# Factor transfers on GpSimd's queue, and finished rows gathered by six transfers a chunk

## The chip, the cores and the metric

The kernel runs on one core of a Trainium2 chip. The metric is the device time of one execution in microseconds (us), as the median of several executions. The engines named are PE (TensorE), DVE (VectorE), ACT (ScalarE), POOL (GpSimd) and SP (SyncE, which here only issues transfers). An engine works through its own instructions in order and waits on semaphores that others raise.

## The reference

A dynamic convolution over seven rows with softmaxed weights is followed by a squared-ReLU feed-forward layer:

```python
w = exp(weight_gen - max(weight_gen, -1)); w = w / (sum(w, -1) + 1e-9)   # (8, 4096, 8 heads, 7 taps)
out = einsum('bshk,bskhg->bshg', w, x_unf)      # x_unf: each row of x with the 6 rows before it
h = out.reshape(32768, 192) @ w_in              # w_in 192 x 2048
r = maximum(h, 0)
return (r * r) @ w_out                          # w_out 2048 x 192
```

All inputs and the output are float32.

## The kernel before

The 32768 rows are laid out as 128 partitions of 256 rows. A chunk is four rows of every partition, 512 tokens; there are 64 chunks, and two chunks share one load of x (a group of eight rows plus six rows of halo, lines 156 and 157). The feed-forward products are made from high and low parts in reduced precision, so that each chunk has many passes on PE.

A chunk is worked on in eight steps j = 0 to 7. In each, PE makes two blocks of `ph` (`mm1`, line 523), ACT applies ReLU and square and rounds to the high part `gh` (lines 540, 547, 551), DVE makes the low part `gl` (line 560), and PE adds the second product into four accumulators `acc` (lines 604, 608, 614). The second product lags two steps behind, so that a chunk's accumulators are finished in step 1 of the next chunk. There ACT and DVE take them over in two pairs (lines 649 and 651); PE cannot begin the next chunk's sums before DVE's second addition on line 651 has released the second pair. I call the end of that second addition **the handover**; from one to the next is a **stretch**, which is a chunk's worth of work. A stretch that begins in an even chunk is called even.

Chunks 6 to 62 are the scaled ones (`is_scaled`): their weights are multiplied by powers of two taken from the size of x, and their results are scaled back at the end. What happens around one handover, in the order in which the engines have it:

- The convolution for the chunk after the current one runs on DVE (products on line 387, sums on line 400). Its last step, `turn`, transposes 32x32 blocks (line 488) just after the handover. SP writes the result to a scratch in DRAM (`xd`, four transfers, line 494), waits for it, and reads it back transposed (`xT`, two transfers, line 499). ACT rounds xT to `xh` (line 428) and DVE makes `xl` (line 431), from step 5 on; these feed the next chunk's `mm1`.
- The finished chunk's sums X are transposed by DVE in two parts (lines 661 and 664; before the second part SP moves 64 partitions, line 653, and DVE adds them, line 663). SP then gathers them into rows, `o_sb`: 4 column blocks times 4 quarters for part 0 and 2 times 4 for part 1, so 24 transfers (line 671). They are issued after xT's two.
- One chunk later `close_scaled` multiplies `o_sb` by the closing factor `x_out` twice (line 680) and stores it with four transfers (`put_out` with reads 3, line 98).
- In every even chunk, in step 2, `factor` makes that closing factor for a group: DVE makes a column of 128 numbers (line 282), SP writes it to DRAM (`fd`, line 284) and reads it back in the order of the partitions that `o_sb` has (`x_out`, four transfers, line 288). The first of the four waits for `fd` to have landed. `factor` stands ahead of `turn` in the recorded order, and SP has the transfers in that order.

The order of all engines is recorded by hand (`at`, `spread`, `plan_conv`, and the loop over chunks and steps); nothing reorders it. The last chunk (63) is computed in another way, and the gather of part 1 of chunk 62 is on GpSimd's queue.

Of the kernel before, what the change touches and what calls it, by code (L numbers as in the profile page):

```python
# [30 lines left out]
def kernel(  # L31
# [9 lines left out]
    nc = tc.nc  # L41
# [4 lines left out]
    P = 128  # L46
    Q = 32
    HALO = K - 1
    R = B * S // P
    PPB = S // R  # L50
    TC = 4
# [4 lines left out]
    D1 = 64  # L56
# [32 lines left out]
    def put_out(c, t0, t1, o_sb, reads):  # L89
        rows = slice(rows_of(c) + t0, rows_of(c) + t1)  # L90
        if reads == 0:
            nc.sync.dma_start(out=out.rearrange("(p r) d -> p r d", r=R)[:, rows, :], in_=o_sb[:, t0:t1])
            return
        if reads == 3:
            v = out.rearrange("(q j r) d -> j q r d", q=P // Q, r=R)
            n = Q // (P // Q)
            for k in range(P // Q):
                nc.sync.dma_start(out=v[k * n:(k + 1) * n, :, rows, :], in_=o_sb[k * Q:(k + 1) * Q, t0:t1])
            return
        v = out.rearrange("(q a b r) d -> q b a r d", q=P // Q, a=2 ** reads, r=R)  # L100
        for q in range(P // Q):
            nc.sync.dma_start(out=v[q, :, :, rows, :], in_=o_sb[q * Q:(q + 1) * Q, t0:t1])
# [7 lines left out]
    def is_scaled(c):  # L110
        return FIRST <= c < NCH - 1
# [21 lines left out]
    def rows_of(c):  # L133
        return (c + CPG if c < CPG else c - CPG if c < 2 * CPG else c) * TC
# [144 lines left out]
    def factor(gi):  # L279
        f = att.tile([P, 1], F32, name="x_fac", bufs=2)  # L280
        x_out[gi] = fo = att.tile([P, 1], F32, name="x_out", bufs=3)
        nc.vector.tensor_tensor(out=f, in0=x_pow[gi], in1=v_unroot, op=ALU.mult)
        fd = dram.tile([P, 1], F32, name="fd")
        nc.sync.dma_start(out=fd, in_=f)
        v = fd.rearrange("(q j) e -> j q e", q=P // Q)
        n = Q // (P // Q)
        for k in range(P // Q):
            nc.sync.dma_start(out=fo[k * Q:(k + 1) * Q], in_=v[k * n:(k + 1) * n])

    def peak_w(k):  # L290
        nc.vector.tensor_reduce(
            out=peaks[:, k:k + 1], in_=W[:, 0, 2 * k:2 * k + 2, :].rearrange("p j w -> p (j w)").bitcast(F32),
            axis=AX.X, op=ALU.max, apply_absolute_value=True,
        )
# [7 lines left out]
    def spread_peaks():  # L302
        dm = dram.tile([P, 2], F32, name="dm")
        pk = coef[:, 4:6]
        nc.vector.tensor_reduce(out=pk, in_=peaks.rearrange("p (w k) -> p w k", w=2), axis=AX.X, op=ALU.max)
        nc.sync.dma_start(out=dm, in_=pk)
        nc.sync.dma_start(out=tops, in_=dm.rearrange("p w -> (p w)").rearrange("(o n) -> o n", o=1).broadcast_to([P, 2 * P]))

    def coefficients():
        ts = nc.vector.tensor_scalar  # L310
        top = coef[:, 4:6]
        nc.vector.tensor_reduce(out=top, in_=tops.rearrange("p (q w) -> p w q", w=2), axis=AX.X, op=ALU.max)
        nc.vector.tensor_scalar_max(top, top, W_MIN)
# [15 lines left out]
    def conv_steps(c, on_pe, moving=False):  # L329
# [15 lines left out]
        def denominators(s):  # L345
            if is_scaled(c):
                nc.vector.tensor_scalar(out=s, in0=s, scalar1=1e-9, scalar2=x_pow[gi], op0=ALU.add, op1=ALU.mult)
            elif c >= N_PE:
                nc.vector.tensor_scalar_add(s, s, 1e-9) if c < FIRST else nc.vector.tensor_scalar(
                    out=s, in0=s, scalar1=1e-9, scalar2=v_root, op0=ALU.add, op1=ALU.mult)  # L350

        def softmax(r):
            w, e, m, s = wf[:, r], ex[:, r], mx[:, r], sm[:, r]
            sh = [P, r.stop - r.start, K]
            return [
                lambda: nc.vector.tensor_reduce(out=m[:, :, 0], in_=w, axis=AX.X, op=ALU.max),
                lambda: tt(out=w, in0=w, in1=m.broadcast_to(sh), op=ALU.subtract),
                lambda: nc.scalar.activation(e, w, AF.Exp),
                lambda: nc.vector.tensor_reduce(out=s[:, :, 0], in_=terms[:, r], axis=AX.X, op=ALU.add),
                lambda: (denominators(s), nc.vector.reciprocal(s, s)),  # L360
# [282 lines left out]
    def sum_turned(c, parts=(1, 0)):  # L643
        acc = accs[c]
        if c not in works:
            works[c] = stage.tile([P, 3, N], F32, name="raw")
        X = works[c]
        for k in parts:
# [5 lines left out]

    def store_turned(c, part):
        X = works[c]
        if part == 0:
            o_sb = op.tile([P, TC, D], F32, name="o_sb", bufs=2)
            Y = stage.tile([P, 2, N], F32, name="raw")
            outs[c] = o_sb, Y  # L660
            nc.vector.transpose(Y[:, 0], X[:, 0])
        else:
            nc.vector.tensor_tensor(out=X[0:D1, 1], in0=X[0:D1, 1], in1=X[0:D1, 2], op=ALU.add)
            nc.vector.transpose(outs[c][1][0:D1, 1], X[0:D1, 1])
        o_sb, Y = outs[c]
        y = Y[:, part].rearrange("p (t q i) -> p q t i" if c < N_PE or is_scaled(c) else "p (q t i) -> p q t i", t=TC, i=Q)
        for e in range(P // Q if part == 0 else D1 // Q):
            d0 = part * P + e * Q
            for q in range(P // Q):
                queue = nc.gpsimd if part and c == NCH - 2 else nc.sync  # L670
                queue.dma_start(  # L671
                    out=o_sb[q * Q:(q + 1) * Q, :, d0:d0 + Q],
                    in_=y[e * Q:(e + 1) * Q, q],
                )
        if part and not is_scaled(c):
            put_out(c, 0, TC, o_sb, 2)

    def close_scaled(c):
        o_sb, f = outs[c][0], x_out[c // CPG]
        nc.vector.tensor_scalar(out=o_sb, in0=o_sb, scalar1=f, scalar2=f, op0=ALU.mult, op1=ALU.mult)  # L680
        put_out(c, 0, TC, o_sb, 3)

    outs = {}
# [19 lines left out]
    def store(c, t0, t1):  # L703
        put_out(c, t0, t1, outs[c][0], 1 if c == 0 else 0)
# [152 lines left out]
    for gi in range(FIRST // CPG, NCH // CPG):  # L857
        at(CPG * gi - 2, 2, lambda gi=gi: measure(gi))
        at(CPG * gi - 2, 3, lambda gi=gi: power(gi))
        at(CPG * gi, 2, lambda gi=gi: factor(gi))  # L860
# [8 lines left out]
    for c in range(1, NCH):  # L869
        tail = c == NCH - 1  # L870
        for j in range(NJ):
# [37 lines left out]
            if c > 1:  # L909
                for part in range(2):  # L910
                    if j == (LOAD_STEP if tail else 2 * part + 2 if is_scaled(c - 1) else OUT_STEP + part):
                        store_turned(c - 1, part)
# [11 lines left out]
    c = NCH - 1  # L924
# [15 lines left out]
    t, end = TC - 1, range(NF - 4, NF)  # L940
# [6 lines left out]
    o_sb, tmp = outs[c]  # L947
# [33 lines left out]
```

## Time and profile before

| | |
|---|---|
| median of three executions | 2494.65 us (2491.42 to 2495.36) |
| the profiled execution | 2495.27 us, of which the span is 2493.5 us |
| mean granted clock of PE | 0.931 |
| busy PE / DVE / ACT / POOL | 2223.0 / 1956.2 / 1843.6 / 14.3 us |
| share of the span PE / DVE / ACT / POOL | 89% / 78% / 74% / 1% |

Busy time of PE is counted at whatever clock was granted, so a slow stretch counts as busy too. The last chain of work alternates between PE, DVE, transfers and SP's queue. "a <- b" in a list of waits means that a's engine stood idle until b was done.

### The profile page before, as it was taken

The page shows a single profiled execution, that of the slowest core. Times are in us where ns is not written, and L with a number is a line of the kernel's source. Part 1 is how long each engine was busy: PE and PEld are TensorE (multiplying, and loading weights), DVE is VectorE, ACT ScalarE, POOL GpSimd, SP SyncE. Part 2 cuts the span into 40 slices and gives each one's busy share as a digit, 9 for nine tenths or more (in the row PEclk, how much of TensorE's full clock was granted, in tenths as well). Part 3 has the DMA queues.
Part 4 walks back from the last instruction along what each step waited for, and adds up shares of the span by engine and source line. Part 5 has one row for each costly group of instructions (what it writes and reads, how often), then busy time and mean ns, then how long its engine had stood idle before and what let it go on. Part 6 is the DMA issues. An engine that isn't in the chain of part 4 may idle for free.

```text
span 2493.5 us, 50277 instructions
## 1 busy us (share of the span) xinstructions
PE 2223.0 (89%) x19484; PEld 1773.6 (71%) x19484; DVE 1956.2 (78%) x3067; ACT 1843.6 (74%) x3551; POOL 14.3 (1%) x26
## 2 busy tenths in 40 slices
PE   9989888898888988989878988899888898888998
PEld 8878666776667766767757766677676776767777
DVE  9988877787777877778777887778877778777784
ACT  8878767787676866768767776677876778767786
POOL 1000000000000000000000000000000000000000
PEclk9999989998899988999999988899998999989999
DMA  8332332323223233232333333333333333333322
GB/s 213 83 87 73 85 66 71 85 72 87 63 71 84 73 73 76 70 86 74 60 77 79 84 80 59 76 80 85 79 60 83 72 85 78 60 84 72 87 51 54
DMA packets 332367, 195.49 MB, mean 78 GB/s; under 512 B 232936, under 2 KB 290536, under 8 KB 328288
## 3 DMA queue, kind: packets, MB, share of 16 engines
q1 hardware_dynamic: 330576, 188.62, 32.1%
q0 software_dynamic: 1552, 3.67, 0.8%
q8 instruction: 152, 2.49, 0.5%
q14 instruction: 87, 0.71, 0.1%
HBM read 106.54 MB, written 49.56 MB: 63 GB/s over the span
## 4 chain that ended last, share of the span: by engine, by line
PE 37%; DVE 26%; DMA 15%; SPq 12%; issue 5%; ACT 5%; DVEq 0%; ACTq 0%
PE ph L523 19%; PE acc L604 11%; SPq L671 9%; DMA xT<-xd 7%; DVE pr L387 6%; DVE gl L560 5%; DVE pr L400 4%; DMA fd<-x_fac 3%; DMA xd<-xr 2%; PE acc L608 2%; DVE raw L651 2%; DMA o_sb<-raw 2%; DVE du L560 2%; DVE xl L431 2%; PE acc L614 2%
## 5 line engine op out<-in xcount | busy, mean ns | idle before, releaser
L523 PE MATMUL ph<-xh,W 64*128 64x512 f32 x6096 | 1094.5, 416 | 4.0 <-ACT xh L428 1.6
L604 PE MATMUL acc<-gh,V 64*128 64x512 f32 x5472 | 838.8, 409 | 250.9 <-ACT gh L551 146.7
L604 PEld LDWEIGHTS acc<-gh,V 64*128 64x128 f32 x5472 | 613.4, 200 | 380.5 <-ACT gh L551 157.9
L523 PEld LDWEIGHTS ph<-xh,W 64*128 64x128 f32 x6096 | 730.9, 194 | 115.0 <-ACT gh L551 16.5
L540 ACT ACTIVATE rg<-ph 128x512 f32<-128x512 f32 x992 | 538.9, 597 | 292.3 <-PE ph L523 287.5
L547 ACT ACTIVATE rg<-rg 128x512 f32<-128x512 f32 x1007 | 581.0, 634 | 4.6 <-DVE rg L536 4.3
L551 ACT CAST gh<-rg 128x512 fp32r<-128x512 f32 x1008 | 575.8, 626 | 3.2 <-PE acc L581 2.9
L523 PE MATMUL ph<-xl,W 64*128 64x512 f32 x3048 | 502.3, 386 | 0.1
L560 DVE TENSOR_TENSOR gl<-rg,gh 128x512 f16<-128x512 f32 x570 | 390.9, 742 | 63.3 <-ACT gh L551 59.8
L387 DVE TENSOR_TENSOR pr<-xt,wt 128x768 f32<-128x768 f32 x440 | 417.8, 951 | 2.2
L431 DVE TENSOR_TENSOR xl<-xT,xh 128x512 fp32r<-128x512 f32 x186 | 122.2, 687 | 375.3 <-ACT xh L428 324.7
L523 PEld LDWEIGHTS ph<-xl,W 64*128 64x128 f32 x3048 | 369.8, 195 | 45.2 <-DVE xl L431 0.5
L400 DVE TENSOR_TENSOR pr<-pr 128x768 f32<-128x768 f32 x366 | 348.6, 952 | 2.2
L428 ACT CAST xh<-xT 128x512 fp32r<-128x512 f32 x186 | 108.0, 618 | 268.1 <-DMA xT<-xd 268.1
L608 PE MATMUL acc<-gl,du 64*128 64x512 f16 x1140 | 249.2, 406 | 0.6 <-DVE gl L560 0.6
L560 DVE TENSOR_TENSOR du<-rg,gh 128x512 f16<-128x512 f32 x342 | 232.3, 733 | 3.7 <-ACT gh L551 3.7
L608 PEld LDWEIGHTS <-du 64*128 64x128 f16 x1824 | 101.6, 101 | 94.1 <-issue 48.0
L608 PE MATMUL acc<-du 64*128 64x512 f16 x684 | 135.6, 418 | 0.8 <-DVE du L560 0.8
L614 PEld LDWEIGHTS <-du 64*64 64x64 f16 x1824 | 48.2, 106 | 57.9 <-issue 24.1
L651 DVE TENSOR_TENSOR raw<-acc,raw 128x512 f32<-128x512 f32 x124 | 84.2, 683 | 5.1 <-ACT raw L649 5.1
L649 ACT COPY raw<-acc 128x512 f32<-128x512 f32 x124 | 74.1, 602 | 13.9 <-PE acc L639 9.3
L639 PE MATMUL acc<-gh,V 64*128 64x512 f32 x480 | 82.4, 381 | 0.0
(126 smaller groups left out, 1076.2 us busy)
## 6 DMA issues: line engine op xcount, KB each, us to landing
xT<-xd SPq DMA_DIRECT2D x124, 384.0 KB
xt<-in_x_dram SPq DMA_DIRECT2D x30, 1344.0 KB
out_dram<-o_sb SPq DMA_DIRECT2D x254, 96.0 KB
xd<-xr SPq DMA_DIRECT2D x248, 96.0 KB
o_sb<-raw SPq DMA_DIRECT2D x1480, 16.0 KB
raw<-raw SPq DMA_DIRECT2D x62, 128.0 KB
wt<-in_weight_gen_dram SPq DMA_DIRECT2D x31, 224.0 KB
raw<-in_moe_w_in_dram SPq DMA_DIRECT2D x16, 192.0 KB
```

Of the source, the lines that this page charges most:

```text
L387: tt(out=dst, in0=src, in1=wf[:, t0 * H:t1 * H, k:k + 1].broadcast_to([P, m, G]), op=ALU.mult)
L400: tt(out=prs[k0], in0=prs[k0], in1=prs.pop(k), op=ALU.add)
L431: tt(out=parts["l"][:, k, n], in0=src[k][:, n], in1=parts["h"][:, k, n].bitcast(F32), op=ALU.subtract)
L523: nc.tensor.matmul(two[i], w, order(xx[rows, k]), start=(n == 0), stop=(n == last))
L540: nc.scalar.activation(r, ph, AF.Relu)
L547: nc.scalar.activation(r, r, AF.Square)
L551: nc.scalar.copy(gh, rgs[c, fb])
L560: nc.vector.tensor_tensor(out=gl, in0=g, in1=h, op=ALU.subtract)
L604: nc.tensor.matmul(acc[b + h], V[rows, fb, e:e + P], two_halves(g[rows]), start=fb == 0 and e < 2 * P, stop=False)
L608: nc.tensor.matmul(acc[h], V16[rows, 2 * j + i, 0:P], gls[c, j][rows, i], start=False, stop=last and i == 1)
L651: nc.vector.tensor_tensor(out=X[:, k], in0=acc[2 * k + 1], in1=X[:, k], op=ALU.add)
L671: queue.dma_start(out=o_sb[q * Q:(q + 1) * Q, :, d0:d0 + Q], in_=y[e * Q:(e + 1) * Q, q],)
```

## The change

Two things change, both for the scaled chunks alone. First, `factor`'s five transfers move from SP's queue to GpSimd's. Second, DVE's transpositions write their 32x32 blocks in another order (all four rows of a quarter side by side: `p (a t i)`), so that one transfer moves a column block of 32 for all 128 partitions; a chunk has six gathers in place of 24, each four times as large. The partition that a token ends in changes with it (4 times the position in the block plus the quarter), so the views through which `put_out` stores and `factor` reads back change as well. Part 1 of chunk 62 goes to SP's queue with the rest.

```diff
         if reads == 3:
-            v = out.rearrange("(q j r) d -> j q r d", q=P // Q, r=R)
-            n = Q // (P // Q)
-            for k in range(P // Q):
-                nc.sync.dma_start(out=v[k * n:(k + 1) * n, :, rows, :], in_=o_sb[k * Q:(k + 1) * Q, t0:t1])
+            v = out.rearrange("(q a b r) d -> b q a r d", q=P // Q, a=P // Q, r=R)
+            n = v.shape[0] // 4
+            for k in range(4):
+                nc.sync.dma_start(out=v[k * n:(k + 1) * n, :, :, rows, :], in_=o_sb[k * Q:(k + 1) * Q, t0:t1])
             return
...
-        nc.sync.dma_start(out=fd, in_=f)
-        v = fd.rearrange("(q j) e -> j q e", q=P // Q)
-        n = Q // (P // Q)
-        for k in range(P // Q):
-            nc.sync.dma_start(out=fo[k * Q:(k + 1) * Q], in_=v[k * n:(k + 1) * n])
+        nc.gpsimd.dma_start(out=fd, in_=f)
+        v = fd.rearrange("(q a b) e -> b q a e", q=P // Q, a=P // Q)
+        n = v.shape[0] // 4
+        for k in range(4):
+            nc.gpsimd.dma_start(out=fo[k * Q:(k + 1) * Q], in_=v[k * n:(k + 1) * n])
...
+        def blocks(v):
+            return v.rearrange("p (a t i) -> p t a i", a=P // Q, t=TC) if is_scaled(c) else v
+
...
-            nc.vector.transpose(Y[:, 0], X[:, 0])
+            nc.vector.transpose(blocks(Y[:, 0]), X[:, 0])
...
-            nc.vector.transpose(outs[c][1][0:D1, 1], X[0:D1, 1])
+            nc.vector.transpose(blocks(outs[c][1][0:D1, 1]), X[0:D1, 1])
...
+            if is_scaled(c):
+                nc.sync.dma_start(out=o_sb[:, :, d0:d0 + Q], in_=outs[c][1][e * Q:(e + 1) * Q, part])
+                continue
```

On SP, two chunks in the middle of the program, from one handover to the one after next. Each row is a transfer (destination <- source, the pieces of the destination, how many such transfers follow each other). Before:

```order
L653 DMA raw<-raw 64x512
L284 DMA fd<-x_fac 128x1
L288 DMA x_out<-fd 32x1x1 x4
L494 DMA xd<-xr 32x6x128 x4
L499 DMA xT<-xd 64x3x512 x2
L671 DMA o_sb<-raw 32x4x32 x24
L98 DMA out_dram<-o_sb 8x4x768 x4
L653 DMA raw<-raw 64x512
L494 DMA xd<-xr 32x6x128 x4
L499 DMA xT<-xd 64x3x512 x2
L671 DMA o_sb<-raw 32x4x32 x24
```

The same place now, on SP:

```order
L653 DMA raw<-raw 64x512
L494 DMA xd<-xr 32x6x128 x4
L499 DMA xT<-xd 64x3x512 x2
L674 DMA o_sb<-raw 128x4x32 x6
L98 DMA out_dram<-o_sb 2x16x768 x4
L653 DMA raw<-raw 64x512
L494 DMA xd<-xr 32x6x128 x4
L499 DMA xT<-xd 64x3x512 x2
L674 DMA o_sb<-raw 128x4x32 x6
```

The two rows of the factor are gone from between the 64 partitions' move and `xd`, the 24 gathers are six, and the store's pieces read 2x16x768 where they read 8x4x768.

On GpSimd, from the early chunks' accumulating transfers (line 405) to the first factors, which stand as the first work of the scaled chunks there now (before, the eight gathers of chunk 62 came next):

```order
L405 DMA pr<-prw 128x768
L284 DMA fd<-x_fac 128x1
L288 DMA x_out<-fd 32x1x1 x4
L284 DMA fd<-x_fac 128x1
L288 DMA x_out<-fd 32x1x1 x4
```

This pair of rows follows 29 times in all, and nothing else stands between them on that queue.

## Rows read from the trace of the kernel before

**Rows 1.** Who waited for whom, whole span: total us, times, longest us.
```profile
ACT xh L428 <- DMA xT<-xd: 268.1, 30, 11.5
PE acc L604 <- ACT gh L551: 146.7, 28, 7.3
PE acc L604 <- DVE raw L651: 101.1, 71, 4.1
```

**Rows 2.** Waits of SP's own queue, whole span.
```profile
SPq L288 <- DMA fd<-x_fac: 204.9, 28, 7.9
```

**Rows 3.** SP's timeline over two stretches: start us, us from first to last issue, transfers.
```profile
1022.28 0.33 SPq L284 DMA_DIRECT2D fd<-x_fac  x1
1029.82 2.77 SPq L288 DMA_DIRECT2D x_out<-fd  x4
1032.69 1.85 SPq L494 DMA_DIRECT2D xd<-xr  x4
1037.25 1.33 SPq L499 DMA_DIRECT2D xT<-xd  x2
...
1038.68 15.88 SPq L671 DMA_DIRECT2D o_sb<-raw  x24
1056.64 3.05 SPq L98 DMA_DIRECT2D out_dram<-o_sb  x4
...
1066.44 1.80 SPq L494 DMA_DIRECT2D xd<-xr  x4
1069.87 1.32 SPq L499 DMA_DIRECT2D xT<-xd  x2
```

**Rows 4.** DVE and ACT in the same stretches: start us, us, work [idle before <- releaser].
```profile
1020.25 0.68 DVE L651 TENSOR_TENSOR raw<-acc,raw 128x512 f32<-128x512 f32 x1
1022.18 0.96 DVE L488 STREAM_TRANSPOSE xr<-pr 128x768 f32<-128x768 f32 x1
...
1043.31 0.62 ACT L428 CAST xh<-xT 128x512 fp32r<-128x512 f32 x1 [9.50 <-DMA xT<-xd]
1043.96 0.69 DVE L431 TENSOR_TENSOR xl<-xT,xh 128x512 fp32r<-128x512 f32 x1 [10.82 <-ACT xh L428]
1055.93 0.68 DVE L680 TENSOR_SCALAR o_sb<-o_sb,x_out 128x768 f32<-128x768 f32 x1 [1.09 <-DMA o_sb<-raw]
1063.57 0.68 DVE L651 TENSOR_TENSOR raw<-acc,raw 128x512 f32<-128x512 f32 x1
...
1079.49 0.62 ACT L428 CAST xh<-xT 128x512 fp32r<-128x512 f32 x1
1080.14 0.69 DVE L431 TENSOR_TENSOR xl<-xT,xh 128x512 fp32r<-128x512 f32 x1 [2.30 <-ACT xh L428]
1098.65 0.68 DVE L651 TENSOR_TENSOR raw<-acc,raw 128x512 f32<-128x512 f32 x1
```

**Rows 5.** PE alone, by stretches cut at its idle gaps: us, busy, clock, DMA, GB/s.
```profile
1062.50:1069.30 6.80, 6.21 (x28) 0.50 0.38 76
1069.30:1098.77 29.47, 29.46 (x284) 1.00 0.41 109
...
1099.39:1117.60 18.21, 18.21 (x165) 1.00 0.22 43
```

**Rows 6.** Line 284 over the whole span: nanoseconds, first and last start.
```profile
L284 SPq DMA_DIRECT2D fd<-x_fac x29: 321/330/348, 241.2 to 2424.5; - x29
```

**Rows 7.** Windows of transfers (store, x load, gather): last three columns PEclk, DMA share, GB/s.
```profile
1058.00:1060.86 2.86, 2.22 (x19) 1.60 (x17) 2.86 (x5) 1.98 (x5) 0.00 (x0) 1.00 0.34 138
1011.81:1016.05 4.24, 4.24 (x45) 3.15 (x45) 4.24 (x7) 3.70 (x8) 0.00 (x0) 1.00 0.94 366
1041.92:1055.47 13.55, 10.97 (x82) 8.65 (x84) 10.88 (x15) 12.16 (x24) 0.00 (x0) 0.75 0.23 33
```

**Rows 8.** Line 671's transfers on POOL: nanoseconds min/median/max, first and last start.
```profile
L671 POOL DMA_DIRECT2D o_sb<-raw x8: 556/556/599, 2472.0 to 2475.8; - x8
```

**Rows 9.** Line 661's transpositions on DVE, 1000 to 1100 us: busy us, mean ns | idle.
```profile
L661 DVE STREAM_TRANSPOSE raw<-raw 128x512 f32<-128x512 f32 x2 | 1.3, 666 | 0.0
```

## The prediction

> **What bounds the kernel now.** I read the list of waits first. PE's idle time has two large entries: it waits for ACT's rounded blocks 28 times for 146.7 us and for DVE's release of the accumulators 71 times for 101.1 us [rows 1]. Above the first stands ACT waiting 30 times, 268.1 us in all, for xT to come back from DRAM. 28 is about once per two chunks, so I looked at who holds xT back only in every other stretch. SP's own list names it: 28 times, 204.9 us, SP stands on line 288 until `fd` has landed [rows 2].
>
> The timelines of two stretches show how this works. Handovers end at 1020.93, 1064.25 and 1099.33 us (each start plus 0.68) [rows 4]; the even stretch takes 43.32 us, the odd one 35.08, together 78.40. In the even one DVE has `xr` ready at 1023.14, but SP issued `fd` at 1022.28, stood until 1029.82, read `x_out` back, and came to `xd` only at 1032.69 [rows 3]. That is 11.76 us after the handover. In the odd one `xd` goes out at 1066.44, 2.19 us after it. So `xd` is late by 9.57 us in the even stretch, and ACT's wait for xT there is 9.50 us [rows 4]: the same time.
>
> The stall is paid again at once. DVE is late by it, so that the next handover finds PE waiting, and PE's granted clock falls to 0.50, its lower level of 1.2 GHz, from 1062.50 to 1069.30 [rows 5]. In the odd stretch PE regains 1.00 and keeps it through the gap of 0.62 us between 1098.77 and 1099.39, on both sides of which the clock is 1.00.
>
> **The change, part by part.**
>
> *Factors off SP.* SP loses `fd`, its wait and four issues between line 653 and `xd`. In both kinds of stretch `xd` can then start 2.2 us after the handover (1066.44 less 1064.25), and the last xT issue ends 6.94 us after it (1069.87 plus 1.32) [rows 3]. From that issue's end to ACT's start the even stretch took 4.73 us (1038.58 to 1043.31) [rows 3, 4], so xT is there 11.7 us after the handover. When is it wanted? In the even stretch ACT stood ready at 1043.31 less 9.50, which is 12.88 us after the handover. In the odd one it took xT 15.24 us after, of which 5.05 us ran at half clock and lost 2.5, so 12.7. xT is in time by about 1.1 us: the stall is covered by PE's own work in steps 2 to 5.
>
> What is late next? DVE. From ACT's `xh` to DVE's `xl` it is 0.65 us, and from `xl` to the next handover DVE works nearly without a pause: 1080.14 to 1099.33, 19.19 us; in the even stretch 20.29, less the 1.09 that it waited for a gather, 19.20 [rows 4]. The loop from handover to handover is therefore 12.9 + 0.65 + 19.2 = 32.75 us in even stretches and 12.7 + 0.65 + 19.2 = 32.55 in odd ones: 65.3 a pair. PE alone needs 5.05 / 2 + 29.47 = 32.0 a stretch at full clock [rows 5], so about 0.65 us of idle PE is left at each handover, as long a gap as the one that leaves the clock at 1.00 now.
>
> Line 284 starts 29 times from 241.2 to 2424.5 us [rows 6]: 28 pairs of 77.98 us on average, each with one stall. 28 x (77.98 - 65.3) = 355 us.
>
> *Factors on GpSimd.* POOL has no other work there. The nearest row is a POOL transfer of 0.56 us [rows 8]; `fd` with the same wait of 7.2 us, then four of these, come to some 12 us. The factor is used by line 680 two handovers later, less some 8 us (1055.93 against 1064.25) [rows 4], which is 57 us on. So I cost it at nothing. If making the transfers held DVE up, it would be at most 5 x 0.6 = 3 us a pair (84 us in all); I take zero, since this falls ahead of `xl`, where DVE is idle anyway (2.30 us in the odd stretch, 10.82 in the even one, of which about 1.3 stays).
>
> *Six gathers for 24.* Pieces and bytes are the same. On SP 24 issues took 15.88 us [rows 3], 0.66 each. Six of them take 4 us if an issue costs the same with four times the pieces, and 16 us as now if it goes by pieces. I take the low end: an `xd` transfer has 32 x 6 = 192 pieces to line 671's 32 x 4 = 128, and its four issues took 1.85 us, so pieces do not set it. The effect is on line 680: its wait of 1.09 us for the gather [rows 4] ends (I have already left it out of the 19.2), and a gather that stayed slow would bring back about 1.1 us a stretch.
>
> *Transpositions.* Line 488, which writes permuted blocks already, takes 0.96 us for 768 columns [rows 4]; line 661, in order, 666 ns for 512 [rows 9]: 1.25 against 1.30 ns a column. Between these bounds the cost is 0.03 us either way; I take none.
>
> *Stores.* Same bytes and issues, other pieces; see the second rival.
>
> *Sum.* 2495.3 (profiled execution, 0.6 over the median) less 355 is 2140. I add 5 us, a tenth of a us for each of 56 stretches, as my choice for transfers less punctual than in the pair that I read: **2145 us**.
>
> **The rivals.**
>
> *First, gathers or xT slower than I take them.* Gathers issued by pieces bring 1.1 us a stretch back; xT late by 2 us rather than early by 1.1 brings 0.9. Either gives up to 2145 + 56 x 1.1 = 2207. For it: the cover of xT is thin. Against it: the odd stretches show that path every time.
>
> *Second, stores on fewer transfer engines.* The store's leading count falls from 8 to 2. A chunk's store keeps 0.34 of 16 engines busy for 2.86 us, 15.6 engine-us [rows 7]. If it ran on eight engines and now runs on two, it lasts 15.6 / 2 = 7.8 us. It begins to move 1.4 us after its issue (1058.00 against 1056.64), 6.2 us before the handover, and `xd` begins no sooner than 2.2 us after it, so up to 8.4 us is free and two engines cost nothing. On one engine, 15.6 us, `xd` and xT would come 7.2 us later; less the 1.1 in hand that is 6 us a stretch, 2145 + 56 x 6 = 2481 or somewhat less. The trace is in keeping with eight before: the store's share of 0.34 stays under one half, the load of x, with 128 pieces in front, reaches 0.94 [rows 7]. The Trainium skill (DMA: Bandwidth & Descriptors, Why a DMA increments its semaphore by 16 and not by 1) says that a transfer uses the largest number of engines, up to 16, that divides the leading size of both sides. By that rule the stores here go from eight engines to two, and the gathers stay on 16. The trace agrees as to eight, by that share of 0.34; no row of before can show two.
>
> *Third, the clock.* If the gap at the handover were long enough that PE falls to 1.2 GHz in each stretch, all would be like the odd one now, 35.08 us: 2495.3 - 28 x (77.98 - 70.2) = 2277. Against it: a gap of 0.62 does not do that [rows 5].
>
> *Fourth, slower: the gather lands on few engines.* One source partition now feeds four destination partitions. The gather's packets take 0.23 x 16 x 13.55 = 50 engine-us [rows 7]. If the new shape ran on two engines, that is 25 us a chunk, beginning about 8.3 us after the handover, and line 680 could start 33.3 us after it plus a landing; from there it is 8.3 us to the handover (1055.93 to 1064.25). The stretch becomes about 42.5 us against 39 now, 2495.3 + 28 x (85 - 77.98) = 2692. It decides from about 21.5 us of gather. Against it: both sides of the new shape begin with 32 or 128 pieces, as transfers do that are fast now.
>
> *Fifth, no change:* something else holds `xd` in the even stretches, and moving the factor frees nothing: 2495. Against it, `xd` follows line 288 by 0.1 us.
>
> **How the numbers follow.** My forecast, 2145 with 2104 as its low end (PE's 32.0 a stretch as the bound: 28 x (77.98 - 64.0) = 391), has 0.70. The first rival has 0.12, the second, where it costs anything, 0.04, the third 0.07, the fourth 0.04, the fifth 0.03. The range takes in the forecast and the first rival: 2104 to 2210. Faster by over 0.2% (5 us, about what a measurement of this kernel can tell from no change) is the first four lines, 0.93; within it the fifth rival, 0.03; slower the fourth, 0.04.
>
> **What would show it.** Right: ACT's wait for xT is nearly gone from the list; SP has `xd` about 2.2 us after every handover; handovers come every 32 to 33 us in even and odd stretches alike; PE's idle is a gap under 1 us before each, and its mean clock is near 1.00; line 680 no longer waits for gathers. Wrong: a wait of ACT for xT in every stretch (transfers crowd: first or second rival), clock 0.50 after handovers (third), line 680 idle for long (fourth), or line 671's successor at 2.4 us an issue.

## The result, and the profile after

The changed kernel takes 2346.73 us (median of four, 2339.68 to 2351.56), against 2495.01 for the kernel before in the same comparison; the ratio is 0.9405 (95% interval 0.9376 to 0.9433). That is faster, as forecast, but by 148 us and not by 350, and outside the range. The profiled execution has a span of 2342.3 us and a mean granted clock of 0.973 (0.931 before).

The lists of waits, of all engines and of SP's queue alone, whole span (total us, times, longest us), show what is left. They answer to [rows 1, 2].

```profile
POOL x_out L288 <- DMA fd<-x_fac: 228.5, 27, 10.1
ACT xh L428 <- DMA xT<-xd: 195.1, 40, 7.6
PE acc L604 <- DVE raw L651: 83.2, 83, 2.1
PE acc L604 <- ACT gh L551: 74.9, 29, 3.5
...
SPq L499 <- DMA xd<-xr: 307.9, 109, 9.6
```

ACT still waits for xT, 195.1 us where it was 268.1. The wait for `fd` is now POOL's, 228.5 us where it was SP's 204.9. And SP has a new one in a place that I had not looked at: between writing `xd` and reading it back it stands 307.9 us in all, up to 9.6 at a time.

Two stretches, odd and then even, on SP (start us, us from first to last issue), then what POOL, ACT and DVE do in them. They answer to [rows 3, 4].

```profile
935.11 1.80 SPq L494 DMA_DIRECT2D xd<-xr  x4
939.77 1.28 SPq L499 DMA_DIRECT2D xT<-xd  x2
941.14 4.94 SPq L674 DMA_DIRECT2D o_sb<-raw  x6
...
968.14 1.81 SPq L494 DMA_DIRECT2D xd<-xr  x4
979.40 1.28 SPq L499 DMA_DIRECT2D xT<-xd  x2
...
967.52 0.59 POOL L284 DMA_DIRECT2D fd<-x_fac  x1 [60.12 <-DVE x_fac L282]
976.43 2.37 POOL L288 DMA_DIRECT2D x_out<-fd  x4 [8.32 <-DMA fd<-x_fac]
...
985.56 0.62 ACT L428 CAST xh<-xT 128x512 fp32r<-128x512 f32 x1 [6.77 <-DMA xT<-xd]
...
932.27 0.68 DVE L651 TENSOR_TENSOR raw<-acc,raw 128x512 f32<-128x512 f32 x1
965.22 0.68 DVE L651 TENSOR_TENSOR raw<-acc,raw 128x512 f32<-128x512 f32 x1
1004.61 0.69 DVE L651 TENSOR_TENSOR raw<-acc,raw 128x512 f32<-128x512 f32 x1
```

The handovers are at 932.95, 965.90 and 1005.30 us: 32.95 us for the odd stretch, 39.40 for the even one. Over the 53 stretches that begin between 310 and 2240 us the means are 33.39 for odd and 39.45 for even ones (35.08 and 43.32 in the pair of before). `xd` now goes out 2.2 us after every handover. But in the even stretch SP ends the four issues at 969.95 and cannot read back before 979.40, 9.5 us later; in the odd one 2.9 us were enough. POOL sees `fd` landed at 976.43.

What the transfer engines do meanwhile is in the window from 971.50 to 976.40 (us, granted clock of PE, busy share of the transfer engines, GB/s):

```profile
971.50:976.40 4.90, 1.00 0.00 0
```

They move nothing. All bytes of `xd` have been moved by then, and SP is still not told that they have landed.

### The profile page after: what moved, and what is told of

It reads as the page before. It is cut to its first block, busy times and chain, and to the rows that moved or that the text cites. A ratio compares the mean times of both kernels' runs of the same rounds, so it can differ in the third digit from the quotient of the medians.

```text
span 2342.3 us, 49184 instructions
## 1 busy us (share of the span) xinstructions
PE 2151.8 (92%) x19484; PEld 1735.2 (74%) x19484; DVE 1949.2 (83%) x3067; ACT 1842.7 (79%) x3551; POOL 95.6 (4%) x163
## 4 chain that ended last, share of the span: by engine, by line
DVE 43%; PE 26%; DMA 17%; ACT 5%; issue 5%; SPq 2%; DVEq 0%; another core or an unknown queue 0%; ACTq 0%
PE ph L523 14%; DVE pr L400 10%; DMA xT<-xd 9%; DVE pr L387 9%; DVE du L560 9%; DMA xd<-xr 7%; PE acc L604 6%; DVE xl L431 4%; DVE gl L560 4%; DVE raw L651 3%; PE acc L639 2%; ACT rg L540 2%; PE acc L608 1%; ACT xh L428 1%; ACT rg L547 1%
## 5 line engine op out<-in xcount | busy, mean ns | idle before, releaser
L523 PE MATMUL ph<-xh,W 64*128 64x512 f32 x6096 | 1066.0, 409 | 0.0
L604 PE MATMUL acc<-gh,V 64*128 64x512 f32 x5472 | 796.2, 393 | 160.2 <-DVE raw L651 83.2
L604 PEld LDWEIGHTS acc<-gh,V 64*128 64x128 f32 x5472 | 593.1, 191 | 276.6 <-DVE raw L651 120.6
L523 PEld LDWEIGHTS ph<-xh,W 64*128 64x128 f32 x6096 | 715.8, 190 | 100.2 <-ACT gh L551 13.2
L523 PE MATMUL ph<-xl,W 64*128 64x512 f32 x3048 | 491.0, 380 | 0.1
L523 PEld LDWEIGHTS ph<-xl,W 64*128 64x128 f32 x3048 | 360.0, 189 | 40.9 <-ACT xl L442 0.5
L428 ACT CAST xh<-xT 128x512 fp32r<-128x512 f32 x186 | 108.0, 618 | 195.1 <-DMA xT<-xd 195.1
L608 PE MATMUL acc<-gl,du 64*128 64x512 f16 x1140 | 237.3, 390 | 1.0 <-DVE gl L560 1.0
L608 PE MATMUL acc<-du 64*128 64x512 f16 x684 | 132.9, 400 | 15.1 <-DVE du L560 14.4
L284 POOL DMA_DIRECT2D fd<-x_fac x29 | 17.1, 589 | 1874.9 <-DVE x_fac L282 1752.4
L614 PEld LDWEIGHTS <-du 64*64 64x64 f16 x1824 | 48.3, 106 | 57.8 <-issue 24.1
```

Of the source, the lines that this page charges most:

```text
L428: nc.scalar.copy(parts["h"][:, k, n], src[k][:, n])
L523: nc.tensor.matmul(two[i], w, order(xx[rows, k]), start=(n == 0), stop=(n == last))
L604: nc.tensor.matmul(acc[b + h], V[rows, fb, e:e + P], two_halves(g[rows]), start=fb == 0 and e < 2 * P, stop=False)
L608: nc.tensor.matmul(acc[h], V16[rows, 2 * j + i, 0:P], gls[c, j][rows, i], start=False, stop=last and i == 1)
```

## The experiments

Theory A: the 128 numbers of `fd`, 4 bytes each, take some 8 us to land in DRAM, and transfers issued behind them are held until then, in whatever queue they were put. Theory B: something else in the even stretch holds `xd`. Theory C: transfers made by GpSimd delay those of SP.

**Later: the factor four steps later.**

```diff
-        at(CPG * gi, 2, lambda gi=gi: factor(gi))
+        at(CPG * gi, 6, lambda gi=gi: factor(gi))
```

> The changed kernel with the factor made four steps later (step 6 of the even chunk in place of step 2), so that xd and xT are out before fd is written; everything else as changed. Theory A (fd's 128 pieces of 4 bytes take some 8 us to land in DRAM, and a transfer that is issued behind them on any queue is not reported done before that): even stretches, 39.45 us on average in the changed kernel, become like its odd ones, 33.4, and SP's wait between xd and xT falls from about 9.5 to 2.9 us; 2347 - 28 x 6.05 = 2178 us. Theory B (something else of the even stretch delays xd, such as the load of x or the measuring of its size): no difference, 2347 us.

Measured: 2141.98 us (2139.88 to 2143.97), ratio to the kernel before 0.8592 (0.8578 to 0.8606). Waits in this kernel:

```profile
POOL x_out L288 <- DMA fd<-x_fac: 197.3, 26, 8.3
PE acc L604 <- DVE raw L651: 39.5, 65, 1.4
...
SPq L499 <- DMA xd<-xr: 107.2, 109, 2.8
```

`fd` still takes 7.6 us to land (197.3 over 26; 8.5 in the changed kernel), but nothing urgent stands behind it, and SP's wait for `xd` is 2.8 us at most. Odd stretches average 32.82 us, even ones 32.68, and the clock 0.997. Theory B falls. The gain beyond the 2178 that I expected comes from both kinds: even stretches fell below the 33.4 that I took from the odd ones, and odd ones got shorter too. A part of their 33.39 was half clock left by the stall before: in the changed kernel 15 of the 23 odd stretches between 310 and 2040 us ran wholly at 1.00 and average 32.89 us, the other 8 hold up to 3.4 us at 0.50 and average 34.15.

**In SBUF: no scratch in DRAM.**

```diff
-        fd = dram.tile([P, 1], F32, name="fd")
-        nc.gpsimd.dma_start(out=fd, in_=f)
-        v = fd.rearrange("(q a b) e -> b q a e", q=P // Q, a=P // Q)
-        n = v.shape[0] // 4
-        for k in range(4):
-            nc.gpsimd.dma_start(out=fo[k * Q:(k + 1) * Q], in_=v[k * n:(k + 1) * n])
+        for b in range(8):
+            nc.gpsimd.dma_start(out=fo[b * 16:(b + 1) * 16], in_=f[b::8])
```

> The changed kernel with the closing factor permuted from SBUF to SBUF by eight transfers of 16 numbers on GpSimd's queue, without the scratch in DRAM, still in step 2. Theory A, in the form that the landing in DRAM is what is slow: even stretches near 33.4 us, 2178 us in all. Theory C (transfers made by GpSimd, whatever they write, delay those of SP): even stretches stay at 39 us or grow, since eight transfers stand ahead, 2347 us or more. If tiny pieces are slow wherever they land, also about 2347.

Measured: 2141.81 us (2141.33 to 2142.38), ratio 0.8589 (0.8576 to 0.8602), in step 2 as in the changed kernel, with eight transfers of GpSimd's and 4-byte pieces ahead of `xd`. SP's wait for `xd` (line 495 is line 499 of the changed kernel):

```profile
SPq L495 <- DMA xd<-xr: 117.7, 113, 3.0
```

Theory C falls, and so does the thought that tiny pieces are slow wherever they land: it is the write to DRAM.

**Padded: the numbers 512 bytes apart.**

```diff
-        fd = dram.tile([P, 1], F32, name="fd")
+        fd = dram.tile([P, 128], F32, name="fd")[:, 0:1]
```

> The changed kernel with the 128 numbers of fd at 512 bytes from one another in DRAM in place of side by side, 4 bytes each as before. Theory A1 (the pieces are slow because they share the same few hundred bytes, one after the other): fd lands in 2 to 3 us, even stretches near 33.4, about 2178 us. Theory A2 (128 pieces of 4 bytes are slow in DRAM wherever they lie): no difference, about 2347 us.

Measured: 2144.25 us (one run). POOL's two steps and its wait between them:

```profile
900.60 0.59 POOL L284 DMA_DIRECT2D fd<-x_fac  x1 [61.29 <-DVE x_fac L282]
902.80 2.36 POOL L288 DMA_DIRECT2D x_out<-fd  x4 [1.61 <-DMA fd<-x_fac]
...
POOL x_out L288 <- DMA fd<-x_fac: 52.8, 27, 3.5
```

For the same 128 pieces of 4 bytes, in the same step, POOL waits 1.6 us here and 2 us on average (52.8 over 27), where side by side they took 8.5 (228.5 over 27). What makes them slow is that they lie side by side, within the same 512 bytes; no run tries a spacing between 4 and 512 bytes. Why that is slow no run here shows.

**Double: fd written twice,** to two scratches.

```diff
+        fd2 = dram.tile([P, 1], F32, name="fd2")
+        nc.gpsimd.dma_start(out=fd2, in_=f)
         nc.gpsimd.dma_start(out=fd, in_=f)
```

> The changed kernel with fd written twice, to two scratches, one behind the other on GpSimd's queue. Theory A, if two such writes follow each other: xT comes 8 us later still in even stretches, 39.45 becomes about 47, 2347 + 28 x 8 = 2571 us. Theory A, if they land side by side: 2347 to 2365 (0.6 us more of issue). Theory B or C: within 20 us of 2347.

Measured: 2356.91 us (one run), 10 more than the changed kernel. Two such writes overlap: POOL's wait for both is 10.1 us on average (231.3 over 23), against 8.5 for one. It fits theory A in its second form and by itself would not have told A from B or C.

**Step 3: what of transfers that write to SBUF?** One step after the changed kernel's place, `fd` comes behind `xd` and just ahead of xT.

```diff
-        at(CPG * gi, 2, lambda gi=gi: factor(gi))
+        at(CPG * gi, 3, lambda gi=gi: factor(gi))
```

> The changed kernel with the factor in step 3 in place of step 2: fd is then issued on GpSimd's queue about when xd has landed, just ahead of xT, which is written to SBUF. Theory A3 (an engine of the transfers reports a later transfer done only behind its share of fd, wherever the later one writes): fd lands about 13.5 us after the handover and xT is reported then or up to 3 us later, against 12.8 when it is wanted; even stretches 33.6 to 36.5, in all 2164 to 2246 us. Theory A4 (only writes to DRAM are held up by fd): xT is in time, 2140 to 2150 us.

Measured: 2340.95 us (one run). The kind of effect is A3's, the size is not: I expected at most 2246. DVE, SP, POOL and ACT in an even stretch whose handover is at 964.85, and the window in which xT begins to move (its last three columns are the granted clock, the busy share of the transfer engines and GB/s):

```profile
964.17 0.68 DVE L651 TENSOR_TENSOR raw<-acc,raw 128x512 f32<-128x512 f32 x1
969.29 0.59 POOL L284 DMA_DIRECT2D fd<-x_fac  x1 [59.41 <-DVE x_pow L274]
970.47 1.28 SPq L499 DMA_DIRECT2D xT<-xd  x2
971.84 12.79 SPq L674 DMA_DIRECT2D o_sb<-raw  x6
978.69 2.36 POOL L288 DMA_DIRECT2D x_out<-fd  x4 [8.81 <-DMA fd<-x_fac]
983.72 0.62 ACT L428 CAST xh<-xT 128x512 fp32r<-128x512 f32 x1 [5.98 <-DMA xT<-xd]
...
971.50:972.50 1.00, 1.00 (x12) 0.87 (x10) 1.00 (x3) 0.56 (x2) 0.00 (x0) 1.00 2.17 43
```

xT's issues stand where they should, yet ACT gets xT at 983.72, 18.9 us after the handover. The share of 2.17 counts packets that are in flight for a long time while only 43 GB/s move: single packets of xT last up to 8.8 us here, where the median of that size was 0.15 us in the kernel before. So the data of a later transfer is held up too, not only its report, and also when it goes to SBUF; the gathers behind xT are dragged along (12.79 us for six issues that take 5).

**Halves of the change alone.** Six gathers with the factor on SP in step 2 (the two words changed back):

```diff
-        nc.gpsimd.dma_start(out=fd, in_=f)
+        nc.sync.dma_start(out=fd, in_=f)
...
-            nc.gpsimd.dma_start(out=fo[k * Q:(k + 1) * Q], in_=v[k * n:(k + 1) * n])
+            nc.sync.dma_start(out=fo[k * Q:(k + 1) * Q], in_=v[k * n:(k + 1) * n])
```

> One half alone: six gathers as changed, the factor's five transfers back on SP's queue in step 2. Theory A (fd lands some 8 us after its issue, whatever the queue; on SP everything behind it also waits for the four reads' issue): the stall of the kernel before returns, even stretches 42 to 43 us, odd ones about 34 without the wait for the gather: 2440 us. Rival (the gain of the change came from the fewer gathers): about 2347 us.

Measured: 2414.7 us (one run), even stretches of 42.0 us and odd ones of 33.3, where I had expected 2440. And the kernel before with the factor's five transfers on GpSimd's queue (the same two words the other way), 24 gathers:

> The other half alone: the kernel before with the factor's five transfers on GpSimd's queue, 24 gathers a chunk. Theory A: xd is held behind fd as in the changed kernel, and line 680 waits 0.6 to 1 us for the slower gathers in each stretch: 2347 + 28 x 1.6 = 2392 us. Rival (the gain came from the fewer gathers): near 2495 us.

Measured: 2410.42 us (one run), even stretches of 40.5 us and odd ones of 34.7, where I had expected 2392. DVE's waits on line 680, in the kernel before and in this one:

```profile
DVE o_sb L680 <- DMA o_sb<-raw: 49.4, 33, 6.3
DVE o_sb L680 <- DMA o_sb<-raw: 48.3, 31, 6.0
```

The kernel before took 2490.08 us beside these two, so one half alone is worth 75 us, the other 80, and together they give 148. In both, `xd` or its report is held by `fd`. What the queue saves is about the four issues behind the landing: with six gathers the even stretch is 2.6 us longer on SP's queue (42.0 against 39.45), and the four reads take 2.6 us there.

**The place alone, and the spacing alone, in the kernel before.** First the factor in step 6 on SP's queue with 24 gathers (the diff of "later", in the kernel before):

> The kernel before with one number changed: the factor made in step 6 in place of step 2, on SP's queue, 24 gathers. Theory A: the stall of 9.5 us a pair is gone, but the 24 gathers keep SP until 23 us after the handover, fd and its reads until 33, the stores until 36, so that the next xd starts about 2 us late, and line 680 waits for gathers as now: 2200 to 2230 us. Rival (the place of the factor does not matter): 2495 us.

Measured: 2296.83 us (one run), slower than I expected by 67 to 97, even stretches of 34.5 us and odd ones of 36.5. SP in it, where it is worst:

```profile
974.80 0.54 SPq L284 DMA_DIRECT2D fd<-x_fac  x1
983.47 3.67 SPq L288 DMA_DIRECT2D x_out<-fd  x4
987.56 2.83 SPq L98 DMA_DIRECT2D out_dram<-o_sb  x4
990.50 0.58 SPq L653 DMA_DIRECT2D raw<-raw  x1
991.17 3.36 SPq L494 DMA_DIRECT2D xd<-xr  x4
```

The handover is at 984.48, so `xd` starts 6.7 us after it, and the odd stretch that begins there is the longest, 39.2 us. On average `xd` starts 4.35 us after the handovers that begin odd stretches, about what I had counted on, so that its start does not account for the miss. Line 680 waits for gathers for 55.0 us (31 times), ACT for xT for 65.4 us, and the mean clock is 0.969; how the 67 us divide among these is open. Still, moving the factor alone is worth 193 us against the 2490.08 of the kernel before. Then 512 bytes between the numbers in the kernel before (the diff of "padded", nothing else):

> The kernel before with one thing changed: the 128 numbers of fd lie 512 bytes apart in DRAM, still written by SP in step 2, with 24 gathers. Theory A1 (pieces that share the same few hundred bytes land one after the other): SP's wait on line 288 falls from 7.2 to about 2 us, xd starts some 6.5 us after the handover in place of 11.8, xT comes about 3 us later than wanted, even stretches 43.4 become 36 to 38; about 2285 us, between 2250 and 2340. Rival (the wait on line 288 is how long a write and its report take in that place): 2495 us.

Measured: 2329.74 us (2323.93 to 2337.84), ratio 0.9323 (0.9292 to 0.9354). SP's wait on line 288, to be held against [rows 2], and the same place in the timeline:

```profile
SPq L288 <- DMA fd<-x_fac: 42.8, 29, 2.8
...
968.56 0.33 SPq L284 DMA_DIRECT2D fd<-x_fac  x1
969.97 2.77 SPq L288 DMA_DIRECT2D x_out<-fd  x4
972.84 1.87 SPq L494 DMA_DIRECT2D xd<-xr  x4
```

The wait is 1.5 us on average (42.8 over 29) in place of 7.3 (204.9 over 28), and the time lies in theory A1's range, near its upper end. One line of layout, without another queue or fewer gathers, gives more than the whole change did (ratio 0.9323 against 0.9405).

**SP's queue, late, with six gathers; and the store on more engines.** Six gathers with the factor on SP's queue, as in the first of the two halves, and in step 6 as in "later":

> Six gathers, the factor on SP's queue as in the kernel before, but made in step 6 of the even chunk, when SP has nothing urgent behind it. Theory A (what counts is that nothing that is waited for stands behind fd): as fast as with GpSimd's queue and step 6, 2142 us within 5. Rival (SP's standing on line 288 costs wherever it is): stores go out up to 3 us later, 0.5 to 3 us a pair, 2156 to 2226 us.

Measured: 2169.85 us (2169.59 to 2173.79), ratio 0.8716 (0.8702 to 0.8731): the rival's range, 28 us over GpSimd's queue in the same step. SP around an even stretch's end (handover at 1008.20, the end of the DVE row):

```profile
1000.61 2.62 SPq L288 DMA_DIRECT2D x_out<-fd  x4
1003.40 2.65 SPq L98 DMA_DIRECT2D out_dram<-o_sb  x4
...
1007.52 0.68 DVE L651 TENSOR_TENSOR raw<-acc,raw 128x512 f32<-128x512 f32 x1
1010.38 1.79 SPq L494 DMA_DIRECT2D xd<-xr  x4
1016.00 1.29 SPq L499 DMA_DIRECT2D xT<-xd  x2
```

`xd` goes out 2.2 us after the handover as always, but lands 3.8 us after its last issue (2.9 on average over the odd stretches, 2.1 in "later"). The stores went out 4.8 us before the handover where it is 7.6 elsewhere, 2.8 us later, and their packets still run at 1014.1. That is the prediction's second rival, the store on two engines, once its cover is gone. To test it, the store in eight transfers of 16 partitions:

```diff
-            for k in range(4):
-                nc.sync.dma_start(out=v[k * n:(k + 1) * n, :, :, rows, :], in_=o_sb[k * Q:(k + 1) * Q, t0:t1])
+            for b in range(v.shape[0]):
+                nc.sync.dma_start(out=v[b, :, :, rows, :], in_=o_sb[b * 16:(b + 1) * 16, t0:t1])
```

> The kernel with six gathers, the factor on SP's queue in step 6, and in addition the store in eight transfers of 16 partitions each (leading count 16) in place of four with leading count 2. If the 28 us that it lost against the same with GpSimd's queue (2170 against 2142) come from stores on two transfer engines that end after the next xd has begun: 2145 us or less, odd stretches 32.7. If they come from SP's being late as such, which four more issues do not mend: 2170 us or more.

Measured: 2145.47 us (2144.35 to 2152.96), ratio 0.8588 (0.8571 to 0.8604). The same store with GpSimd's queue:

> The kernel with the factor on GpSimd's queue in step 6 and the store in eight transfers of leading count 16. If stores on two engines end some 2 us after the handover and hold up a part of xd and xT there (the stretches of 33 to 33.6 us among those of 32.6): 2135 us, all stretches 32.6. If they are hidden: 2142 us within 3.

Measured: 2143.63 us (2138.99 to 2147.66), ratio 0.8574 (0.8558 to 0.8589): the same as without it. Windows inside the store, of the changed kernel and of the last one (after the us the granted clock, the busy share of the transfer engines and GB/s), against [rows 7]:

```profile
960.50:966.90 6.40, 1.00 0.14 50
...
958.20:961.50 3.30, 1.00 0.47 95
```

A share of 0.14 is two engines and a little (2 of 16 is 0.125), at 50 GB/s; the 128 packets of a chunk's store run from 959.6 to 968.3 us, never more than four at once, where the store on eight or more engines took 2.9 (kernel before) and 3.8 (here). The store on two is free where it is issued 7.6 us before the handover, as it is throughout the changed kernel and "later", and costs about one us a pair where it is issued 3 us later.

## Why the prediction was wrong, point by point

- **What bounds the kernel, and the stall:** right. All of it hangs on xT in even stretches, and once xT is free the kernel runs as the sum said: 2142 us in "later" and "in SBUF" against 2145, stretches of 32.7 to 32.8 against 32.55 to 32.75, PE's idle gap at a handover about 0.62 us at full clock. The first rival's "xT late by 2 us rather than early by 1.1 brings 0.9" holds only for 2 us counted from the 11.7 at which I had xT arrive, since 1.1 of them are in hand.
- **Factors off SP:** here the prediction failed. "`xd` can then start 2.2 us after the handover" was right; "the last xT issue ends 6.94 us after it" was taken from the odd stretch, where no `fd` is on its way. In even stretches it ends 14.8 us after in the one shown (979.40 plus 1.28, less 965.90), and 14.4 on average. I read the 7.2 us between lines 284 and 288 as a wait of SP's queue that ends when the transfers move to another one. It was the time that the write itself needs, on SP's queue as on GpSimd's, and `xd`, issued behind it on another queue, is held with it. I had a row to doubt it by: `fd` is 512 bytes and stood 7.2 us, while `xd`, 384 KB, landed in 2.7 us [rows 3].
- **Factors on GpSimd, "I cost it at nothing":** the cover for the factor's own consumer was right (57 us; line 687 never waits), but `fd` goes out ahead of `xd`, and I had no rival for that. The one closest, the first, let ACT wait 0.9 us for xT; it waited 6.77 in the stretch shown. (The "some 12 us" for the factor on POOL is wrong as a sum: its terms give 10.0, and it took 11.3, from 967.52 to 978.80; nothing hung on it.) The cost is 28 x (39.45 - 32.75) = 188 us in even stretches and 28 x (33.39 - 32.55) = 24 in odd ones, together 212, which is all of the 207 by which the sum's 2140 missed. Of the 24 some 14 are half clock behind the stall (33.39 against 32.89 without it); the other 10 stand in "later" as well.
- **Six gathers for 24:** right as to the issues and the wait. Six issues took 4.94 us against the 4 that I took, and line 680 (687 now) no longer waits. With 24 gathers on the same queues the kernel is 64 us slower (2410.4 against 2346.7), which agrees with the 1.1 us for each of 56 stretches only by luck: line 680's 48.3 us come in 31 waits, one in each even stretch and nearly none in odd ones. The odd stretches are 1.3 us longer all the same, and hold 4.2 us at half clock on average against 1.1 in the changed kernel.
- **Transpositions:** right, 682 ns where 666 stood [rows 9].
- **Second rival, stores on two engines:** its mechanism is real, and it lasts 8.7 us where 7.8 were worked out and 8.4 counted as free. That it costs nothing is shown in "later", where the wide store changes nothing (2143.63 against 2141.98). The rule of the Trainium skill (DMA: Bandwidth & Descriptors, Why a DMA increments its semaphore by 16 and not by 1) is borne out by the share of 0.14.
- **Third to fifth rival:** handovers of themselves did not bring the clock down, which is 0.997 on average in "later"; gathers did not slow down; the time moved, so that the factor in front of `xd` was what held it.

## What to carry to other kernels

When a wait in a queue is long, ask whether the queue waits for a slow transfer or makes it slow: compare the transfer's landing with that of others of its size before moving it. Another queue did not take the slow transfer out of the way of the rest here: `fd` on GpSimd's queue held `xd` on SP's. Put such a transfer where nothing urgent follows, or remove what makes it slow, which here was one line (numbers 512 bytes apart) or the scratch in DRAM as a whole. A cover is a distance in time: the store on two engines was free until something made it start 3 us later.

## What the runs showed of the hardware

- 128 pieces of 4 bytes written side by side into 512 bytes of DRAM land in about 8 us (POOL waits 8.5 on average, SP 7.3); 512 bytes apart the waits are 2.0 and 1.5, and written to SBUF the pieces hold up nothing (SP's wait for `xd` at most 3.0 us).
- `xd`, issued behind them on SP's queue, is not reported before them, whether they are on SP's queue or on GpSimd's. The trace records the single counts by which a transfer is reported done, up to 16 for one. In the changed kernel the first counts for `fd` come at 970.52, 971.56 and 972.34 us, and those for the first transfer of `xd` at 970.70, 971.74 and 972.52, each within 0.2 us, though the last packet of `xd` had moved by 971.16. The Trainium skill (DMA: Bandwidth & Descriptors, Queues, rings and completion order) says that an engine's report of a transfer comes only after its earlier writes, across queues; these counts agree. In "step 3" later packets themselves last up to 8.8 us behind such a write.
- Open: SP is told of `xd` 3 us after POOL is told of `fd` (979.40 against 976.43); the last counts of its third and fourth transfer come together between 978.98 and 979.35, and no run says what they waited for. POOL issues the four reads of `x_out` in that time (976.43 to 978.80).
